# Retention followed by a SwiGLU layer on one core: the first chunk's pieces in another order, and the normalised rows written a slot ahead of their transposes

## Chip, core and metric

The kernel runs on one core of a Trainium2 chip. The metric is device time in microseconds (us) of one launch, lower is better. Engines are named as in the profile: PE (TensorE matmul), PEld (its weight load), DVE (VectorE), ACT (ScalarE), POOL (GpSimd), SP (SyncE, which here only issues transfers).

## What is computed

```python
def _attn_ref(q, k, v):                      # 4 batches, 8 heads, 768 positions, 64 wide
    for t in range(S):
        state = gamma * state + einsum('bhd,bhe->bhde', k[:, :, t], v[:, :, t])
        y[:, :, t] = scale * einsum('bhd,bhde->bhe', q[:, :, t], state)
...
x = y.transpose(0, 2, 1, 3).reshape(B * S, H * D)          # 3072 x 512
xn = x / sqrt(mean(x * x) + 1e-6) * rms_g
out = (silu(xn @ w_gate) * (xn @ w_val)) @ w_out           # 512 -> 1536 -> 512
```

All inputs and the output are float32; the kernel multiplies in bf16.

## The kernel before

The sequence is cut into 6 chunks of 128 positions. For each chunk c there are two kinds of work. The **attention pieces** run once for each of the 4 batches b:

- `cast` (line 132): q and k to bf16 (`qb`, `kb`), v times a decay (`vp`). In chunk 0 `qb` is made by ACT (line 139), in the others by POOL (line 141); `kb` and `vp` are POOL's (lines 142 and 143).
- `piece_t`: eight PE transposes into the PSUM tile `qk_ps`, one ACT copy to `qkT` (line 158).
- `piece_a`: eight matmuls into two PSUM tiles `a_ps`, two DVE multiplications by the causal mask into `am` (line 172).
- `piece_y`: the matmuls for `y_ps` and for the state's increment `kv_ps`, the DVE multiplication that gives `x` (line 199), ACT's square sum `xsq` (line 203), POOL's `ms` and `rstd` (lines 220 and 223), and the state: in chunk 0 ACT copies it to `st_f` (line 212), later DVE adds to it (line 214); POOL casts it to `st_b` (line 215).
- `piece_x`: DVE writes `xn` (line 229), PE transposes it into `xt_ps` (line 232), DVE multiplies by `g_col` into `xnT` (line 233).

The **feed-forward slots** of chunk c are 16: slots 0 to 11 are `gv(n)` (four matmuls into `g_ps`, line 264, four into `v_ps`, line 267, ACT's silu `sg`, line 269, DVE's product `hT`, line 270), slots 12 to 15 are `down(b)` (twelve matmuls into `o_ps`, line 275, ACT's copy `o_sb`, line 278, a transfer out on SP, line 279). Below, FFN(c) is this stage for chunk c, and g(n) is slot n's first matmul.

The order on every engine is the order in which the program is written: nothing is rescheduled. Chunk 0's pieces come first, in the order of a string of steps (letters C, T, A, Y, X with a batch number). Then, in each slot of FFN(c), the table `PLAN` says which pieces of chunk c+1 follow that slot's own work (`PLAN1` for chunk 1):

```python
PLAN = dict(cast=(0, 2, 4, 6), t=(1, 3, 5, 7), a=(2, 4, 6, 8), y=(3, 5, 7, 9), x=(9, 11, 13, 14))
```

Transfers in: q, k and v of one chunk and batch are three transfers of 256 KB on SP (`load`, line 64), twelve for a chunk. Chunk 0's are issued first of all; chunk 1's four groups each wait for the silu of slot 0 to 3 of FFN(0) (line 269's result, `mark`); chunk 2's follow chunk 1's on SP, and only behind them stands the first transfer out. The weights come in bf16 through POOL's queue: four pairs of 384 KB transfers for `wg_b` and `wv_b` (`load_w`, lines 122 and 123; a pair serves three slots) and three of 512 KB for `wo_b` (`load_wo`, line 127). Before, pair 0 is issued behind batch 1's cast, pair 1 behind batch 2's, pair 2 behind batch 3's, pair 3 and `wo_b` after all of chunk 0's pieces but the last `X`. Eight matmuls into a tile `hot` (line 298) stand ahead of that last `X`.

Of the kernel before, what the change touches and what calls it, by code (L numbers as in the profile page):

```python
# [17 lines left out]
def kernel(  # L18
# [11 lines left out]
    nc = tc.nc  # L30
# [3 lines left out]
    C = 128  # L34
# [3 lines left out]
    DFF = moe_w_gate.shape[1]  # L38
    KS = DM // 128
# [20 lines left out]
    def load(c, b, after=None):  # L60
        t = []
        for name, src in (("q_f", q), ("k_f", k), ("v_f", v)):
            x = loads.tile([128, H, D], F32, name=name)
            i = nc.sync.dma_start(  # L64
                out=x, in_=src[b].rearrange("h (c p) d -> c p h d", p=C)[c])
            if after is not None:
                tc.add_manual_dep(i.ins, after.ins.name, SYNC_DEP, reason="transfer order")
            t.append(x)
        raw[c, b] = t

    for b in range(B):
# [8 lines left out]
        out=causal, in_=causal, compare_op=ALU.is_ge, fill=0.0, base=0,  # L80
# [18 lines left out]
    warm = const.tile([128, 1], F32, name="warm")  # L99
    nc.scalar.activation(warm, zero, AF.Silu)  # L100
    g_col = const.tile([128, KS], F32, name="g_col")
    for s in range(KS):
        nc.scalar.dma_start(out=g_col[:, s:s + 1], in_=moe_rms_g[s * 128:(s + 1) * 128][:, None])


    st_f = [const.tile([128, NHP, D], F32, name=f"st_f{b}") for b in range(B)]
    st_b = [const.tile([128, NHP, 2 * D], BF16, name=f"st_b{b}") for b in range(B)]
# [22 lines left out]
    cur = {}  # L130
    mark = {}

    def cast(c, b):
        q_f, k_f, v_f = raw.pop((c, b))
        qb = work.tile([128, DM], BF16, name="qb")
        kb = work.tile([128, DM], BF16, name="kb")
        vp = work.tile([128, H, D], BF16, name="vp")
        if c == 0:
            nc.scalar.copy(qb, q_f.rearrange("p h d -> p (h d)"))  # L139
        else:  # L140
            nc.gpsimd.tensor_copy(qb, q_f.rearrange("p h d -> p (h d)"))
        nc.gpsimd.tensor_copy(kb, k_f.rearrange("p h d -> p (h d)"))  # L142
        nc.gpsimd.tensor_tensor(  # L143
            out=vp, in0=v_f, in1=vdec[:, c, :, None].to_broadcast([128, H, D]), op=ALU.mult)
        cur[c, b] = dict(qb=qb, kb=kb, vp=vp)
        if c == 0 and b > 0:
            load_w(b - 1)
        if 0 < c < NCH - 1:
            load(c + 1, b)

# [26 lines left out]
    def piece_y(c, b):  # L177
        d = cur[c, b]
        y_ps = aps.tile([128, H, D], F32, name="y_ps", tag="at")
        first = True  # L180
        for hp in range(NHP):
            for i in range(2):
                h = 2 * hp + i
                last = c == 0 and h == H - 1
                nc.tensor.matmul(y_ps[:, h, :], d["am"][:, i, hp, :], d["vp"][:, h, :],  # L185
                                 start=first, stop=last, skip_group_check=True)
                first = False
        if c > 0:
# [12 lines left out]
        xsq = work.tile([128, DM], F32, name="xsq")
        ssq = work.tile([128, 1], F32, name="ssq")
        nc.scalar.activation(xsq, x.rearrange("p h d -> p (h d)"), AF.Square,  # L203
                             accum_out=ssq)
        d["ssq"] = ssq
        piece_rstd(c, b)
        if c < NCH - 1:
            for i in range(2):
                r = slice(i * 64, i * 64 + 64)
                kv = kv_ps[r, :, i * 64:i * 64 + 64]  # L210
                if c == 0:
                    nc.scalar.copy(st_f[b][r], kv)
                else:
                    nc.vector.tensor_tensor(out=st_f[b][r], in0=st_f[b][r], in1=kv, op=ALU.add)
                nc.gpsimd.tensor_copy(st_b[b][r, :, i * 64:i * 64 + 64], st_f[b][r])  # L215
        d["x"] = x

    def piece_rstd(c, b):
        ms = work.tile([128, 1], F32, name="ms")
        nc.gpsimd.tensor_scalar(out=ms, in0=cur[c, b]["ssq"], scalar1=1.0 / DM, scalar2=1e-6,  # L220
                                op0=ALU.mult, op1=ALU.add)
        rstd = work.tile([128, 1], F32, name="rstd")
        nc.gpsimd.tensor_tensor(out=rstd, in0=ms, in1=mhalf, op=ALU.pow)  # L223
        cur[c, b]["rstd"] = rstd
# [114 lines left out]
```

## Time and profile before

| what | us |
|---|---|
| median of 3 runs (lowest to highest) | 295.89 (295.15 to 296.45) |
| the profiled execution, its own time | 295.43 |
| its span in the profile | 293.4 |
| PE busy | 242.3 (83%) |
| DVE busy | 135.3 (46%) |
| ACT busy | 105.6 (36%) |
| POOL busy | 96.1 (33%) |

The span is the stretch that the profile covers; the 2.0 us between it and the execution's own time lie around it. An engine's busy time is the sum of its instructions. In the timeline a line gives start, duration, engine, line of the program, operation, output from inputs, how many were merged, and in brackets the idle time before it on its engine with what ended it. "SPq" and "ACTq" lines are issues of transfers, not the transfers themselves.

### The profile page before, as it was taken

What the parts mean: (1) busy time and instruction counts of PE and PEld (TensorE: products, weight loads), DVE (VectorE), ACT (ScalarE), POOL (GpSimd) and SP (SyncE); (2) the same over time, 40 slices, a digit from 0 to 9 for tenths busy, and PEclk for the clock granted to TensorE, in tenths of its full rate; (3) what the DMA queues carried; (4) which work ended last, traced back from release to release, by engine and by line L of the source; (5) the groups of instructions that cost most, each with busy time, mean ns of one, the idle gap of its engine ahead of it and who ended that gap; (6) DMA issues with size and microseconds to landing.
All of it is one profiled execution on the core that took longest, in us unless ns stands there. A gap on an engine that the chain in (4) does not pass through costs nothing.

```text
span 293.4 us, 4497 instructions
## 1 busy us (share of the span) xinstructions
PE 242.3 (83%) x1673; PEld 123.9 (42%) x1704; DVE 135.3 (46%) x224; ACT 105.6 (36%) x199; POOL 96.1 (33%) x184
## 2 busy tenths in 40 slices
PE   0364798699939998899996899996999978999994
PEld 0243443255514544345443445443454434444441
DVE  0156433266634757326676426576324665224300
ACT  8255233243323463123642124642135432233311
POOL 6457620364270462600653400654301611000000
PEclk9999999799969999999999999999999999999999
DMA  9999699999999400028920129900120000110012
GB/s 166 208 162 122 96 175 196 231 203 216 251 198 218 74 2 0 36 91 193 221 35 1 38 107 223 209 2 0 68 78 2 0 0 2 71 71 3 0 45 98
DMA packets 84741, 30.17 MB, mean 103 GB/s; under 512 B 76016, under 2 KB 81648, under 8 KB 84720
## 3 DMA queue, kind: packets, MB, share of 16 engines
q1 hardware_dynamic: 78336, 25.17, 42.0%
q0 software_dynamic: 5808, 4.72, 10.5%
q8 instruction: 13, 0.21, 0.3%
q10 hardware_dynamic: 576, 0.00, 0.1%
q14 instruction: 8, 0.07, 0.1%
HBM read 28.31 MB, written 6.29 MB: 118 GB/s over the span
## 4 chain that ended last, share of the span: by engine, by line
PE 51%; DVE 17%; ACT 10%; DMA 8%; issue 7%; POOL 4%; SPq 2%; ACTq 0%; DVEq 0%; POOLq 0%
PE o_ps L275 19%; PE v_ps L267 11%; PE g_ps L264 11%; DVE am L172 6%; DMA k_f<-in_k_dram 5%; ACT xsq L203 4%; DVE hT L270 4%; DVE x L199 4%; ACT qkT L158 3%; ACT sg L269 3%; PE xt_ps L232 3%; DVE xn L229 2%; DMA v_f<-in_v_dram 2%; PE qk_ps L156 2%; SPq L64 2%
## 5 line engine op out<-in xcount | busy, mean ns | idle before, releaser
L270 DVE TENSOR_TENSOR hT<-sg,v_ps 128x512 bf16<-128x512 bf16 x72 | 49.5, 688 | 86.0 <-PE v_ps L267 61.5
L264 PE MATMUL g_ps<-xnT,wg_b 128*128 128x512 bf16 x272 | 73.4, 386 | 2.8 <-DVE xnT L233 1.6
L267 PE MATMUL v_ps<-xnT,wv_b 128*128 128x512 bf16 x281 | 74.9, 385 | 0.6
L269 ACT ACTIVATE sg<-g_ps 128x512 bf16<-128x512 f32 x72 | 43.0, 597 | 60.2 <-PE g_ps L264 58.2
L275 PE MATMUL o_ps<-wo_b,hT 128*128 128x512 bf16 x281 | 63.9, 379 | 0.5 <-issue 0.2
L220 POOL TENSOR_SCALAR ms<-ssq 128x1 f32<-128x1 f32 x24 | 4.8, 202 | 123.8 <-ACT xsq L203 123.8
L267 PEld LDWEIGHTS <-wv_b 128*128 128x128 bf16 x288 | 28.5, 99 | 35.1 <-issue 1.9
L275 PEld LDWEIGHTS <-hT 128*128 128x128 bf16 x288 | 27.4, 98 | 30.4
L264 PEld LDWEIGHTS <-wg_b 128*128 128x128 bf16 x288 | 26.2, 99 | 29.0 <-issue 4.0
L172 DVE TENSOR_TENSOR am<-a_ps,causal 128x512 bf16<-128x512 f32 x48 | 30.8, 683 | 16.5 <-PE a_ps L168 16.3
L278 ACT COPY o_sb<-o_ps 128x512 f32<-128x512 f32 x24 | 14.1, 586 | 62.5 <-PE o_ps L275 58.1
L233 DVE TENSOR_TENSOR xnT<-xt_ps,g_col 128x512 bf16<-128x512 bf16 x24 | 16.6, 692 | 36.3 <-PE xt_ps L232 36.3
L203 ACT ACTIVATE xsq<-x 128x512 f32<-128x512 f32 x24 | 15.1, 630 | 43.9 <-DVE x L199 43.9
L158 ACT COPY qkT<-qk_ps 128x1024 bf16<-128x1024 bf16 x24 | 24.0, 1000 | 13.5 <-PE qk_ps L156 13.5
L143 POOL TENSOR_TENSOR vp<-v_f,vdec 128x512 bf16<-128x512 f32 x24 | 25.3, 1053 | 3.5 <-DMA v_f<-in_v_dram 3.5
L232 PE MATMUL xt_ps<-ident,xn 128*128 128x128 bf16 x96 | 10.3, 235 | 17.4 <-DVE xn L229 17.4
L156 PE MATMUL qk_ps<-ident,qb 128*128 128x128 bf16 x96 | 10.2, 234 | 15.0 <-ACT qb L139 15.0
L232 PEld LDWEIGHTS <-xn 128*128 128x128 bf16 x96 | 7.1, 105 | 24.9 <-DVE xn L229 22.2
L142 POOL CAST kb<-k_f 128x512 bf16<-128x512 f32 x24 | 15.1, 627 | 6.5 <-DMA k_f<-in_k_dram 6.4
L199 DVE TENSOR_TENSOR x<-y_ps,ydec 128x512 f32<-128x512 f32 x24 | 16.5, 686 | 1.0 <-PE y_ps L185 0.7
L229 DVE TENSOR_SCALAR xn<-x,rstd 128x512 bf16<-128x512 f32 x24 | 14.6, 609 | 4.4 <-POOL rstd L223 4.4
L215 POOL CAST st_b<-st_f 64x256 bf16<-64x256 f32 x40 | 16.2, 406 | 1.2
(41 smaller groups left out, 162.1 us busy)
## 6 DMA issues: line engine op xcount, KB each, us to landing
q_f<-in_q_dram SPq DMA_DIRECT2D x24, 256.0 KB, 5.1
k_f<-in_k_dram SPq DMA_DIRECT2D x24, 256.0 KB, 5.1
v_f<-in_v_dram SPq DMA_DIRECT2D x24, 256.0 KB, 5.1
out_dram<-o_sb SPq DMA_DIRECT2D x24, 256.0 KB, 2.0
wg_b<-in_moe_w_gate_dram POOLq DMA_DIRECT2D x4, 384.0 KB, 5.5
wv_b<-in_moe_w_val_dram POOLq DMA_DIRECT2D x4, 384.0 KB, 6.5
wo_b<-in_moe_w_out_dram POOLq DMA_DIRECT2D x3, 512.0 KB, 12.0
g_col<-in_moe_rms_g_dram ACTq DMA_DIRECT2D x4, 0.5 KB, 4.0
```

The source lines that it names most:

```text
L143: nc.gpsimd.tensor_tensor(out=vp, in0=v_f, in1=vdec[:, c, :, None].to_broadcast([128, H, D]), op=ALU.mult)
L158: nc.scalar.copy(qkT, qk_ps)
L172: nc.vector.tensor_tensor(out=am[:, i], in0=a_ps[i], in1=causal[:, None, :].to_broadcast([128, NHP, 128]), op=ALU.mult)
L199: nc.vector.tensor_tensor(out=x, in0=y_ps, in1=ydec[:, c, :, None].to_broadcast([128, H, D]), op=ALU.mult)
L203: nc.scalar.activation(xsq, x.rearrange("p h d -> p (h d)"), AF.Square, accum_out=ssq)
L229: nc.vector.tensor_scalar_mul(xn, d["x"].rearrange("p h d -> p (h d)"), d["rstd"])
L232: nc.tensor.transpose(xt_ps[:, s, :], xn[:, s * 128:(s + 1) * 128], ident)
L264: nc.tensor.matmul(g_ps, wg_b[:, s, sl], xnT[:, s, :], start=s == 0, stop=s == KS - 1)
L267: nc.tensor.matmul(v_ps, wv_b[:, s, sl], xnT[:, s, :], start=s == 0, stop=s == KS - 1)
L269: mark[c, n] = nc.scalar.activation(sg, g_ps, AF.Silu)
L270: nc.vector.tensor_tensor(out=hT[:, n, :], in0=sg, in1=v_ps, op=ALU.mult)
L275: nc.tensor.matmul(o_ps, hT[:, n, b * C:(b + 1) * C], wo_b[:, n, :], start=n == 0, stop=n == NFF - 1)
```

## The change

Five edits. (1) `g_col` comes with one transfer on POOL's queue, called in the string of steps behind batch 1's cast, instead of four on ACT's. (2) In chunk 0, `qb` is cast by DVE instead of ACT, and `st_b` is copied from PSUM by ACT instead of cast from `st_f` by POOL. (3) The weights' pairs are steps of the string: pairs 0 and 1 behind batch 2's cast, pairs 2 and 3 behind batch 3's. (4) `piece_x` is split: `piece_n` writes `xn`, `piece_x` only transposes it and writes `xnT`; in chunk 0's string and in the two tables the first stands ahead of the second, in the tables by one slot (for some batches of chunk 1 in the same one), and the pieces `x` of batches 0 to 2 stand two slots earlier than before in `PLAN`. In chunk 0's string the transposes move back too: `X0` from ahead of `Y1` to behind `A2`, `X1` from ahead of `Y2` to behind `A3`, `X2` from ahead of `Y3` to behind it. (5) The matmuls into `hot` are six, not eight. In `PLAN1` batch 0's cast moves from slot 6 to slot 5.

```diff
-    for s in range(KS):
-        nc.scalar.dma_start(out=g_col[:, s:s + 1], in_=moe_rms_g[s * 128:(s + 1) * 128][:, None])
+    def load_g():
+            nc.gpsimd.dma_start(out=g_col, in_=moe_rms_g.rearrange("(s p) -> p s", p=128))
...
         if c == 0:
-            nc.scalar.copy(qb, q_f.rearrange("p h d -> p (h d)"))
+            nc.vector.tensor_copy(qb, q_f.rearrange("p h d -> p (h d)"))
...
-        if c == 0 and b > 0:
-            load_w(b - 1)
...
                 if c == 0:
+                    nc.scalar.copy(st_b[b][r, :, i * 64:i * 64 + 64], kv)
                     nc.scalar.copy(st_f[b][r], kv)
                 else:
                     nc.vector.tensor_tensor(out=st_f[b][r], in0=st_f[b][r], in1=kv, op=ALU.add)
-                nc.gpsimd.tensor_copy(st_b[b][r, :, i * 64:i * 64 + 64], st_f[b][r])
+                    nc.gpsimd.tensor_copy(st_b[b][r, :, i * 64:i * 64 + 64], st_f[b][r])
...
-    def piece_x(c, b):
-        d = cur.pop((c, b))
+    def piece_n(c, b):
+        d = cur[c, b]
         xn = work.tile([128, DM], BF16, name="xn")
         nc.vector.tensor_scalar_mul(xn, d["x"].rearrange("p h d -> p (h d)"), d["rstd"])
+        d["xn"] = xn
+    def piece_x(c, b):
+        xn = cur.pop((c, b))["xn"]
...
-    PLAN = dict(cast=(0, 2, 4, 6), t=(1, 3, 5, 7), a=(2, 4, 6, 8), y=(3, 5, 7, 9), x=(9, 11, 13, 14))
-    PLAN1 = dict(cast=(6, 7, 9, 11), t=(7, 9, 11, 13), a=(8, 10, 12, 14), y=(9, 11, 13, 15), x=(13, 14, 15, 15))
+    PLAN = dict(cast=(0, 2, 4, 6), t=(1, 3, 5, 7), a=(2, 4, 6, 8), y=(3, 5, 7, 9), n=(6, 8, 10, 13), x=(7, 9, 11, 14))
+    PLAN1 = dict(cast=(5, 7, 9, 11), t=(7, 9, 11, 13), a=(8, 10, 12, 14), y=(9, 11, 13, 15), n=(12, 14, 15, 15), x=(13, 15, 15, 15))
...
-    for step in "C0 T0 C1 A0 T1 Y0 C2 A1 T2 X0 Y1 C3 A2 T3 X1 Y2 A3 X2 Y3".split():
+    for step in ("C0 T0 C1 G0 A0 T1 Y0 C2 W0 W1 A1 T2 Y1 N0 C3 W2 W3 A2 X0 T3 Y2 N1 A3 X1 Y3 N2 X2").split():
         P[step[0]](0, int(step[1]))
-    for i in range(3, DFF // WB):
-        load_w(i)
     for i in range(3):
         load_wo(i)
     hot = fps.tile([128, GT], F32, name="hot", tag="ff")
-    for i in range(8):
+    for i in range(6):
         nc.tensor.matmul(hot, ident, st_b[0].rearrange("p a b -> p (a b)"), start=True, stop=True)
+    piece_n(0, 3)
     piece_x(0, 3)
```

The order on POOL in chunk 0, from batch 1's `vp` on. Before:

```order
L143 TENSOR_TENSOR vp<-v_f,vdec 128x512
L122 DMA wg_b<-in_moe_w_gate_dram 128x4x384
L123 DMA wv_b<-in_moe_w_val_dram 128x4x384
L220 TENSOR_SCALAR ms<-ssq 128x1
L223 TENSOR_TENSOR rstd<-ms,mhalf 128x1
L215 CAST st_b_146<-st_f_142 64x4x64 x2
L142 CAST kb<-k_f 128x512
L143 TENSOR_TENSOR vp<-v_f,vdec 128x512
L122 DMA wg_b<-in_moe_w_gate_dram 128x4x384
L123 DMA wv_b<-in_moe_w_val_dram 128x4x384
```

And with the change:

```order
L146 TENSOR_TENSOR vp<-v_f,vdec 128x512
L105 DMA g_col<-in_moe_rms_g_dram 128x4x1
L222 TENSOR_SCALAR ms<-ssq 128x1
L225 TENSOR_TENSOR rstd<-ms,mhalf 128x1
L145 CAST kb<-k_f 128x512
L146 TENSOR_TENSOR vp<-v_f,vdec 128x512
L125 DMA wg_b<-in_moe_w_gate_dram 128x4x384
L126 DMA wv_b<-in_moe_w_val_dram 128x4x384
L125 DMA wg_b<-in_moe_w_gate_dram 128x4x384
L126 DMA wv_b<-in_moe_w_val_dram 128x4x384
```

The first pair of weights has moved behind batch 2's `vp` and the second pair directly behind it; the casts of `st_b` are gone from POOL, and `g_col`'s transfer is new there. Behind these rows come batch 1's `ms` and `rstd`, batch 3's `kb` and `vp`, and pairs 2 and 3 in the same way.

The order on DVE in slots 6 to 9 of FFN(2), where chunk 3's batches 2 and 3 pass through (`am`, `x`, `st_f` are theirs, the `xn` and `xnT` those of batches 0 and 1). Before:

```order
L270 TENSOR_TENSOR hT<-sg,v_ps 128x512
L172 TENSOR_TENSOR am<-a_ps_1756,causal 128x512
L172 TENSOR_TENSOR am<-a_ps_1757,causal 128x512
L270 TENSOR_TENSOR hT<-sg,v_ps 128x512
L199 TENSOR_TENSOR x<-y_ps,ydec 128x512
L214 TENSOR_TENSOR st_f_144<-st_f_144,kv_ps 64x256 x2
L270 TENSOR_TENSOR hT<-sg,v_ps 128x512
L172 TENSOR_TENSOR am<-a_ps_1849,causal 128x512
L172 TENSOR_TENSOR am<-a_ps_1850,causal 128x512
L270 TENSOR_TENSOR hT<-sg,v_ps 128x512
L229 TENSOR_SCALAR xn<-x,rstd 128x512
L233 TENSOR_TENSOR xnT<-xt_ps,g_col 128x4x128
```

And with the change:

```order
L276 TENSOR_TENSOR hT<-sg,v_ps 128x512
L231 TENSOR_SCALAR xn<-x,rstd 128x512
L173 TENSOR_TENSOR am<-a_ps_1753,causal 128x512
L173 TENSOR_TENSOR am<-a_ps_1754,causal 128x512
L276 TENSOR_TENSOR hT<-sg,v_ps 128x512
L239 TENSOR_TENSOR xnT<-xt_ps,g_col 128x4x128
L200 TENSOR_TENSOR x<-y_ps,ydec 128x512
L216 TENSOR_TENSOR st_f_140<-st_f_140,kv_ps 64x256 x2
L276 TENSOR_TENSOR hT<-sg,v_ps 128x512
L231 TENSOR_SCALAR xn<-x,rstd 128x512
L173 TENSOR_TENSOR am<-a_ps_1854,causal 128x512
L173 TENSOR_TENSOR am<-a_ps_1855,causal 128x512
```

Batch 0's `xn` now stands ahead of batch 2's masks and its `xnT` ahead of batch 2's `x`; batch 1's `xn` and `xnT` stand in the same way in slots 8 and 9, where before they came in slot 11.

## Rows read from the trace of the kernel before

**Rows 1.** Windows: stretch, busy time of each engine, granted clock, DMA share, GB/s.
```profile
1.90:13.40 11.50, 1.22 (x12) 0.96 (x14) 0.00 (x0) 6.67 (x22) 7.19 (x15) 1.00 1.30 216
...
20.60:23.20 2.60, 1.78 (x24) 1.32 (x22) 2.08 (x4) 1.86 (x4) 1.89 (x4) 1.00 0.10 6
23.20:33.20 10.00, 5.66 (x51) 4.17 (x53) 5.57 (x9) 4.26 (x11) 6.30 (x12) 1.00 1.09 157
33.20:36.80 3.60, 2.82 (x13) 1.18 (x12) 1.29 (x2) 0.67 (x2) 3.38 (x7) 1.00 0.11 3
36.80:51.00 14.20, 13.42 (x65) 6.02 (x64) 5.50 (x8) 4.78 (x8) 2.54 (x4) 1.00 1.18 187
51.00:77.00 26.00, 22.01 (x182) 11.90 (x187) 13.12 (x23) 9.82 (x17) 12.99 (x23) 0.93 1.17 214
```

**Rows 2.** Timeline, end of FFN(0) and start of FFN(1).
```profile
76.69 2.76 PE L275 MATMUL o_ps<-wo_b,hT 128*128 128x512 bf16 x12
...
77.14 5.04 SPq L279 DMA_DIRECT2D out_dram<-o_sb  x4
...
81.23 0.59 ACT L278 COPY o_sb<-o_ps 128x512 f32<-128x512 f32 x1 [4.41 <-DMA out_dram<-o_sb]
...
85.50 0.58 PE L264 MATMUL g_ps<-xnT,wg_b 128*128 128x512 bf16 x1 [0.78 <-DVE xnT L233]
```

**Rows 3.** Waits of PE from 86 to 260 us: total, times, longest.
```profile
PE xt_ps L232 <- DVE xn L229: 11.4, 8, 2.4
```

**Rows 4.** Timeline, chunk 0: ACT and what it hands over.
```profile
8.75 1.61 ACTq L103 DMA_DIRECT2D g_col<-in_moe_rms_g_dram  x2
...
10.41 0.62 ACT L139 CAST qb<-q_f 128x512 bf16<-128x512 f32 x1 [3.41 <-DMA v_f<-in_v_dram]
...
17.30 0.74 ACT L212 COPY st_f<-kv_ps 64x256 f32<-64x256 f32 x2
...
18.29 0.93 POOL L215 CAST st_b<-st_f 64x256 bf16<-64x256 f32 x2
```

**Rows 5.** Timeline, slots 8 to 11 of FFN(2): masks, xn, transposes.
```profile
153.23 1.28 DVE L172 TENSOR_TENSOR am<-a_ps,causal 128x512 bf16<-128x512 f32 x2
...
155.09 0.48 DVE L229 TENSOR_SCALAR xn<-x,rstd 128x512 bf16<-128x512 f32 x1
155.63 0.40 PE L232 MATMUL xt_ps<-ident,xn 128*128 128x128 bf16 x4 [1.25 <-DVE xn L229]
155.86 0.40 PE L185 MATMUL y_ps<-vp,am 128*128 128x64 bf16 x8
156.06 0.69 DVE L233 TENSOR_TENSOR xnT<-xt_ps,g_col 128x512 bf16<-128x512 bf16 x1 [0.49 <-PE xt_ps L232]
```

**Rows 6.** Timeline, chunk 0: batch 3's cast on POOL, the last weights, start of FFN(0).
```profile
23.43 0.56 POOL L223 TENSOR_TENSOR rstd<-ms,mhalf 128x1 f32<-128x1 f32 x1
...
24.95 0.61 POOL L142 CAST kb<-k_f 128x512 bf16<-128x512 f32 x1
25.53 1.04 POOL L143 TENSOR_TENSOR vp<-v_f,vdec 128x512 bf16<-128x512 f32 x1
...
32.04 2.34 PE L298 MATMUL hot<-st_b,ident 128*128 128x512 bf16 x5 [0.22 <-issue]
...
34.93 0.81 POOL L122 DMA_DIRECT2D wg_b<-in_moe_w_gate_dram  x1
...
35.75 0.75 POOL L123 DMA_DIRECT2D wv_b<-in_moe_w_val_dram  x1
36.08 1.02 PE L264 MATMUL g_ps<-xnT,wg_b 128*128 128x512 bf16 x4 [0.78 <-DVE xnT L233]
```

**Rows 7.** Instructions that write xn, whole span: count, least, median, most ns.
```profile
L229 DVE TENSOR_SCALAR xn<-x,rstd x24: 477/538/1251, 18.4 to 253.8; 128x512 bf16<-128x512 f32 x24
```

**Rows 8.** Timeline, slot 11 of FFN(2): POOL's vp beside DVE's xn.
```profile
161.16 1.04 POOL L143 TENSOR_TENSOR vp<-v_f,vdec 128x512 bf16<-128x512 f32 x1
161.23 1.25 DVE L229 TENSOR_SCALAR xn<-x,rstd 128x512 bf16<-128x512 f32 x1
```

More of the change, by code (lines that the diff above doesn't have):

```diff
@@ L101 @@
     g_col = const.tile([128, KS], F32, name="g_col")
-    for s in range(KS):
-        nc.scalar.dma_start(out=g_col[:, s:s + 1], in_=moe_rms_g[s * 128:(s + 1) * 128][:, None])
+    def load_g():
+        with nc.allow_non_contiguous_dma(reason="one column per 128 entries"):
+            nc.gpsimd.dma_start(out=g_col, in_=moe_rms_g.rearrange("(s p) -> p s", p=128))
     st_f = [const.tile([128, NHP, D], F32, name=f"st_f{b}") for b in range(B)]
@@ L247, in attention @@
         plan = PLAN1 if c == 1 else PLAN
-        pieces = dict(cast=cast, t=piece_t, a=piece_a, y=piece_y, x=piece_x)
+        pieces = dict(cast=cast, t=piece_t, a=piece_a, y=piece_y, n=piece_n, x=piece_x)
         for b in range(B):
@@ L288 @@
     begin(0)
-    P = dict(C=cast, T=piece_t, A=piece_a, Y=piece_y, X=piece_x)
-    for step in "C0 T0 C1 A0 T1 Y0 C2 A1 T2 X0 Y1 C3 A2 T3 X1 Y2 A3 X2 Y3".split():
+    P = dict(C=cast, T=piece_t, A=piece_a, Y=piece_y, N=piece_n, X=piece_x, W=lambda c, i: load_w(i), G=lambda c, i: load_g())
+    for step in ("C0 T0 C1 G0 A0 T1 Y0 C2 W0 W1 A1 T2 Y1 N0 C3 W2 W3 A2 X0 T3 Y2 N1 A3 X1 Y3 N2 X2").split():
         P[step[0]](0, int(step[1]))
-    for i in range(3, DFF // WB):
-        load_w(i)
     for i in range(3):
```

## The prediction

> **What bounds the kernel now.** I read the transfers' share of each stretch first, then the waits that end last at each stage's edge, then PE's waits in the later chunks.
>
> The first 77 us are a stream of transfers. While the stream runs it moves 187 to 216 GB/s, and in two stretches it stands still: from 20.6 to 23.2 at 6 GB/s and from 33.2 to 36.8 at 3 GB/s, with a thinner stretch of 157 GB/s between them [rows 1]. That stream, not PE, sets the start of FFN(1): SP issues the first transfer out, which stands behind chunk 2's last transfer in, at 77.14; the fourth copy to `o_sb` needs that one's buffer and starts at 81.23 after 4.41 us of waiting, though PE's last `o_ps` ended at 79.45 (76.69 + 2.76); behind that copy on ACT stand the last batch's square sum and so its `rstd`, `xn`, `xnT`, and g(0) of FFN(1) at 85.50 [rows 2]. So FFN(1) moves as the stream moves, as long as PE's own path stays ahead of it.
>
> From there on PE is the bound, and its largest wait is for `xn`: 11.4 us in 8 waits, two in each of FFN(1) to FFN(4) [rows 3]. The first of each pair is about 1.25 us, which leaves 6.4 for the second ones.
>
> **The change, part by part.**
>
> *The head of ACT's queue.* ACT's first cast of `qb` starts at 10.41, just as its last two issues of `g_col` end (8.75 + 1.61 = 10.36) [rows 4]. With one transfer on POOL and the cast on DVE, chunk 0's first transposes no longer stand behind them. The four casts, 0.62 us each on ACT, cost on DVE between 0.48 (its `xn`, the same size and types) and 0.69 (its product `xnT`) [rows 5]; I take 0.5 by the nearer row. On POOL the new issue costs about what a weight's does, 0.75 to 0.81 [rows 6]. Per batch POOL loses the two casts of `st_b` (0.93), and ACT, which copied `st_f` in 0.74, copies twice as much, so +0.74 [rows 4]. All this lies in front of FFN(0) and counts only through its start.
>
> *Start of FFN(0).* Chunk 0's twelve transfers of 0.262 MB still come at 216 GB/s from 1.9 us on [rows 1]: batch 2's nine are there at about 1.9 + 10.9 = 12.8, taken as 13.9 with the time to land. Then POOL does batch 2's `vp` (1.04), pairs 0 and 1 (twice 0.81 + 0.75 = 3.1), `ms` and `rstd` (0.56 for the second, about 0.8 for both), batch 3's `kb` (0.61) and `vp` (1.04): ends at 20.5. Before, that `vp` ended at 25.53 + 1.04 = 26.57 and FFN(0) began 9.5 later, at 36.08 [rows 6]. The steps in these 9.5 are the same in kind (issue of a pair, two `rstd`, `xn`, transposes, `hot`), now with two pairs instead of one (+1.6) and two `hot` fewer (2.34 / 5 = 0.47 each, -0.9). So FFN(0) starts at 20.5 + 9.5 + 0.7 = 30.7, some 5 us earlier. This is not what I book.
>
> *The stream.* Pair 0 is now issued at about 15, while chunk 0's last transfers still run, and pair 1 follows directly: 1.57 MB (pairs of 0.786) at 187 GB/s last to 23.4. Pairs 2 and 3 are issued from 20.5, before the first two are through, and last to 32; `wo_b` is issued at 27 to 30, before that. Chunk 1's transfers wait for the silu of slot 0, at about 32.5, while `wo_b` is under way. So neither gap has a place left. At 187 GB/s the two gaps are worth 2.6 x (1 - 6/187) = 2.5 and 3.6 x (1 - 3/187) = 3.5, and the thin stretch 10.0 x (1 - 157/187) = 1.6 [rows 1]: 7.6 us. Lower bound 6.0 (the gaps alone), upper bound 9.4 (if what follows runs at 214 instead of 187 as well, 14.2 x 27/214 = 1.8 more). I take **7.6**, since 187 is the rate of the weights themselves.
>
> Does PE's path stay ahead? From FFN(0)'s start to FFN(1)'s it took 85.50 - 36.08 = 49.4, of which 81.23 - 79.45 = 1.8 was the wait for the transfer alone. From 30.7 that gives 30.7 + 47.6 = 78.3 at worst, and 77.9 is what the stream allows (85.5 - 7.6). The path also holds waits for chunk 1's transfers, which now land earlier by more than FFN(0) does, so it should come in below. The margin is thin.
>
> *Cast of chunk 1's batch 0 a slot earlier, `n` and `x` in `PLAN1`:* nothing, they end in the same wait at FFN(0)'s end; were the stream faster still, that cover would go and DVE's three transposed batches in slot 15 would come next, about 0.7 each.
>
> *`xn` ahead of its transposes, chunks 2 to 5.* The transposes find `xn` ready, and the eight waits go. But DVE now does `xn` (0.48) ahead of the masks of batch 2 and `xnT` (0.69, spaced 0.61) ahead of its `x`, then `xn` again ahead of batch 3's masks. These stand in a ring: masks, `y_ps`, `x`, square sum, the copy to `qkT` behind it on ACT, the next `a_ps`, the next masks. So batch 3's masks, which ended at 153.23 + 1.28 = 154.51, end at 154.51 + 0.5 + 0.6 + 0.5 = 156.1; `y_ps`, which waited behind the transposes until 155.86, can then start at 156.1 [rows 5]. The first wait of each pair is paid back in full, plus 0.2. The second goes, but the transposes still follow an `xn` that stands behind its slot's `hT`, some 0.2 late. So each FFN gains its second wait less 0.45: 6.4 - 4 x 0.45 = **4.6** us.
>
> The bounds: a gain of 11.4 if the work ahead of the masks costs nothing, and a loss if each of those two `xn` meets POOL's `vp`: one that did took 1.25 instead of 0.48 and ended with it [rows 8]. Twice 0.77 in four FFNs is 6.2, against 4.6 a loss of 1.6. I stay near the middle because such meetings are few: the median `xn` took 0.538 [rows 7].
>
> *The lock between DVE and POOL.* One `xn` waited until POOL's `vp` had ended [rows 8]. The new DVE casts and `xn` stand beside POOL's weight issues in chunk 0, which no row of before shows. If an issue and such a cast hold each other up by that same 0.77, a few meetings delay FFN(0) by 1 to 3 us. The Trainium skill, page "SBUF — State Buffer", section "SBUF: two separate sides", goes further and speaks against this change: a float32 copy inside SBUF on DVE locks POOL out of its port, so that a transfer issued there, about 620 ns alone, takes about 3100. By its figure, an estimate from that page, eight issues would cost 20 us more, FFN(0) would start near 51, and the kernel would take about 304. Nothing in the trace of before shows that size; the `xn` above shows only that the later one waits for the earlier.
>
> *Sum.* 295.43 - 7.6 - 4.6 = 283.2 for the profiled execution. It stood 0.46 below the median of the runs, so **283.7**.
>
> **The rivals.**
>
> - *DVE takes the second gain.* The chain in slots 6 to 9 grows by more than a microsecond in each FFN and nothing of the 4.6 is left. For it: batch 2 and 3's `am` and `x` are on the ring, and each gets DVE work put in front. Against it: 2.4 us of the longest wait lie in slot 11, behind the ring. Time 295.9 - 7.6 = 288.3.
> - *The stream's gaps close only in part.* Pairs 2 and 3 are issued behind batch 3's `vp`; if that ends later than 23.4, the stream stands again, a microsecond for each, and a late FFN(0) brings PE's path to the front in the same way. For it: the margins are 3 us and under 1. The gain then is about 4: 295.9 - 4 - 4.6 = 287.3.
> - *Slower: the port lock.* The eight issues of weights on POOL are held up by DVE's casts and `xn`, and batch 3's `kb`, `vp` and two `rstd` stand behind them. FFN(0) starts 8 d later than 30.7 if each issue grows by d. With PE's path of 49.4 - 1.8 behind it and the 4.6 still gained, the kernel is slower than before from 30.7 + 8d + 47.6 > 85.5 + 4.6, that is d over 1.5 us, an issue of 2.3 instead of 0.8 [rows 6]. At d = 2 it is 295.9 + 4.2 = 300.1. The Trainium skill's rule above is this case at d = 2.5. Against it: the 0.77 seen [rows 8] is half of what decides, and DVE has only three casts and two `xn` among the issues.
> - *The change does nothing:* only if gaps and waits come back elsewhere in full; I see no place.
>
> **How the numbers follow.** The forecast has 0.66 (within 279 to 286), DVE's chain 0.15, the partial stream 0.13, the lock 0.04, nothing 0.02. The range reaches down to 279.0, where the stream gives 9.4 and the second part 7.5 of its 11.4, and up to 289.5, past both milder rivals with 1 us of their own bounds. Beyond lie the lock and the tails of the others, under 2 in 10. About 0.5% (1.5 us) is what a measurement of this kernel can tell from no change: faster 0.94, same 0.02, slower 0.04.
>
> **What would show it.** Right: no stretch under 100 GB/s between 3 and 65 us; FFN(0) near 31; the first transfer out issued near 69.5; FFN(1) near 78; one short wait for `xn` in each later FFN, with `y_ps` of batch 3 as late against g(9) as before. Wrong: weight issues on POOL over 1.5 us (the lock); a standing stream around 24 (late pairs); PE waits for `am` of over half a microsecond in slots 7 and 9 (DVE's chain); FFN(1) not earlier than 82.

## The result and the profile after

| | before | changed |
|---|---|---|
| median of 4 runs, us | 296.07 (295.15 to 296.45) | **280.31** (279.49 to 280.64) |
| profiled execution, its span | 295.43, 293.4 | 279.49, 277.8 |
| FFN(0) to FFN(5) start at | 36.08, 85.50, 129.99, 173.57, 216.15, 258.39 | 29.43, 76.31, 119.38, 160.35, 201.32, 242.94 |

The ratio is 0.947, with a 95% interval of 0.944 to 0.950: faster by 15.8 us, 3.4 us below the forecast and inside its range. Of the kernels run later, one execution of `e2_old_weight_steps` (286.60) fell into a slower state and is left out of its time. The starts (g(0) of each stage, from the timeline) split it: FFN(1) begins 9.19 us earlier, where the stream term had 7.6. The stages FFN(1) to FFN(4) are shorter by 1.42, 2.61, 1.61 and 0.62, together 6.26, where the `xn` term had 4.6.

The windows of the changed kernel, in the stretches of [rows 1] as far as its stream goes (columns as there):

```profile
1.90:13.40 11.50, 4.97 (x48) 3.26 (x48) 4.46 (x8) 8.60 (x27) 7.46 (x17) 1.00 1.27 219
20.60:23.20 2.60, 1.81 (x17) 0.95 (x15) 2.32 (x5) 2.50 (x7) 2.60 (x4) 1.00 1.33 208
23.20:33.20 10.00, 8.35 (x35) 3.84 (x36) 3.71 (x8) 2.65 (x8) 4.18 (x8) 1.00 1.31 202
33.20:36.80 3.60, 3.60 (x18) 1.65 (x17) 1.52 (x3) 1.19 (x2) 0.00 (x0) 1.00 1.23 202
36.80:51.00 14.20, 13.90 (x96) 6.98 (x94) 6.78 (x11) 5.09 (x8) 4.54 (x6) 1.00 1.15 213
51.00:67.00 16.00, 15.56 (x132) 8.09 (x130) 9.57 (x19) 7.72 (x14) 9.32 (x18) 1.00 1.07 213
```

The last column is the reading: no stretch stands still. 6, 157 and 3 GB/s have become 208, 202 and 202, and 187 has become 213. The table leaves out 13.4 to 20.6 us; the thinnest two microseconds in it, 16 to 18, have 145 GB/s.

The timeline of the changed kernel where FFN(0) ends, against [rows 2]:

```profile
66.54 2.76 PE L281 MATMUL o_ps<-wo_b,hT 128*128 128x512 bf16 x12
...
67.93 5.04 SPq L285 DMA_DIRECT2D out_dram<-o_sb  x4
...
71.75 0.68 DVE L200 TENSOR_TENSOR x<-y_ps,ydec 128x512 f32<-128x512 f32 x1
72.02 0.59 ACT L284 COPY o_sb<-o_ps 128x512 f32<-128x512 f32 x1 [5.12 <-DMA out_dram<-o_sb]
...
76.31 1.87 PE L270 MATMUL g_ps<-xnT,wg_b 128*128 128x512 bf16 x4 [0.78 <-DVE xnT L239]
```

The first transfer out is issued 9.21 us earlier (77.14 to 67.93), and FFN(1) follows by the same amount. PE's last `o_ps` ends at 69.30, but the fourth copy still waits for a buffer until 72.02. (The 5.12 in its bracket is all the time that ACT stood idle before it.)

Its timeline in chunk 0, against [rows 4, 6]:

```profile
4.13 0.43 DVE L142 CAST qb<-q_f 128x512 bf16<-128x512 f32 x1 [4.13 <-DMA q_f<-in_q_dram]
...
6.91 0.99 ACT L159 COPY qkT<-qk_ps 128x1024 bf16<-128x1024 bf16 x1
...
14.76 0.82 POOL L125 DMA_DIRECT2D wg_b<-in_moe_w_gate_dram  x1
...
15.43 0.48 DVE L231 TENSOR_SCALAR xn<-x,rstd 128x512 bf16<-128x512 f32 x1
15.59 0.96 POOL L126 DMA_DIRECT2D wv_b<-in_moe_w_val_dram  x1
15.83 0.42 DVE L142 CAST qb<-q_f 128x512 bf16<-128x512 f32 x1
...
19.48 1.03 POOL L146 TENSOR_TENSOR vp<-v_f,vdec 128x512 bf16<-128x512 f32 x1
...
29.43 1.86 PE L270 MATMUL g_ps<-xnT,wg_b 128*128 128x512 bf16 x4 [0.78 <-DVE xnT L239]
```

Two things: the first weights are issued at 14.76, and an issue beside DVE's `xn` and cast takes 0.96, not several microseconds.

PE's waits from 86 to 260 us in the kernel before, beside those of [rows 3], then from 76 to 244 us in the changed kernel, and all its `xn`, against [rows 7]:

```profile
PE a_ps L168 <- ACT qkT L158: 2.0, 6, 0.5
PE y_ps L185 <- DVE am L172: 1.3, 8, 0.2
```

```profile
PE a_ps L169 <- ACT qkT L159: 3.9, 9, 0.7
PE y_ps L186 <- DVE am L173: 3.8, 13, 0.4
...
PE xt_ps L238 <- DVE xn L231: 0.3, 2, 0.2
```

```profile
L231 DVE TENSOR_SCALAR xn<-x,rstd x24: 475/486/1362, 15.4 to 233.3; 128x512 bf16<-128x512 f32 x24
```

The 11.4 us of waits for `xn` are down to 0.3. The waits for `qkT` and for the masks, 2.0 and 1.3 before, are 3.9 and 3.8: part of the gain was paid back there.

### The profile page after: what moved, and what is told of

The parts are those of the page before. It is cut to its first block, busy times and chain, and to the rows that moved or that the text cites. A ratio compares the mean times of both kernels' runs of the same rounds, so it can differ in the third digit from the quotient of the medians.

```text
span 277.8 us, 4510 instructions
## 1 busy us (share of the span) xinstructions
PE 246.2 (89%) x1702; PEld 124.4 (45%) x1702; DVE 135.7 (49%) x228; ACT 105.3 (38%) x203; POOL 94.5 (34%) x177
## 4 chain that ended last, share of the span: by engine, by line
PE 51%; DVE 15%; ACT 9%; DMA 8%; POOL 6%; issue 6%; SPq 3%; ACTq 0%; POOLq 0%; DVEq 0%
PE o_ps L281 21%; PE g_ps L270 13%; PE v_ps L273 12%; DVE am L173 5%; DMA k_f<-in_k_dram 4%; DVE hT L276 3%; SPq L64 3%; ACT xsq L204 3%; DVE x L200 3%; ACT qkT L159 3%; ACT sg L275 3%; DVE xn L231 2%; DMA v_f<-in_v_dram 2%; DVE xnT L239 2%; PE xt_ps L238 2%
## 5 line engine op out<-in xcount | busy, mean ns | idle before, releaser
L270 PE MATMUL g_ps<-xnT,wg_b 128*128 128x512 bf16 x288 | 76.3, 388 | 1.6 <-DVE xnT L239 1.6
L273 PE MATMUL v_ps<-xnT,wv_b 128*128 128x512 bf16 x288 | 75.7, 386 | 0.0
L144 POOL CAST qb<-q_f 128x512 bf16<-128x512 f32 x20 | 12.8, 640 | 15.0 <-DMA q_f<-in_q_dram 14.1
L186 PE MATMUL y_ps<-vp,am 128*128 128x64 bf16 x192 | 13.1, 202 | 4.5 <-DVE am L173 4.5
L169 PE MATMUL a_ps<-qkT 64*128 64x128 bf16 x192 | 10.4, 233 | 6.7 <-ACT qkT L159 6.1
L231 DVE TENSOR_SCALAR xn<-x,rstd 128x512 bf16<-128x512 f32 x24 | 15.6, 649 | 1.1 <-POOL rstd L225 1.1
```

The costliest lines, as they stand in the source:

```text
L270: nc.tensor.matmul(g_ps, wg_b[:, s, sl], xnT[:, s, :], start=s == 0, stop=s == KS - 1)
L273: nc.tensor.matmul(v_ps, wv_b[:, s, sl], xnT[:, s, :], start=s == 0, stop=s == KS - 1)
```

## The experiments

Twelve kernels ran, each beside the kernel before on the same chip. All but one start from the changed kernel; times are medians, to be set against 280.31. The kernel before took 295.04 to 296.07 in the four groups of runs, so a difference of 1 us between times of different groups is not told apart; the ratio is to the kernel before of the same group.

**The old slots for `xn`** (`e1_old_plan`): everything but the split in `PLAN` and the two slots that `x` moved with it.

```diff
-    PLAN = dict(..., n=(6, 8, 10, 13), x=(7, 9, 11, 14))
+    PLAN = dict(..., n=(9, 11, 13, 14), x=(9, 11, 13, 14))
```

> The changed kernel, but in chunks 2 to 5 xn is written in the same slot as its transposes, in the slots of before (9, 11, 13, 14). If the split of xn is worth what FFN(1) to FFN(4) lost in length between the two traces (44.5 to 43.1, 43.6 to 41.0, 42.6 to 41.0, 42.2 to 41.6, together 6.3 us), this takes 280.3 + 6.3 = 286.6 and the two waits for xn stand in each of these stages again. If those stages became shorter for another reason (transfers out of the way, POOL's queue shorter), it takes under 283.

285.38 (284.60 to 286.24), ratio 0.964 [0.961, 0.968]. FFN(1) starts at 76.81, nearly as in the changed kernel; the four stages after it are 4.63 us longer (0.81, 1.60, 1.60, 0.62), which is the forecast's 4.6. Its waits of PE from 76 to 244 us:

```profile
PE xt_ps L238 <- DVE xn L231: 10.3, 8, 1.4
PE a_ps L169 <- ACT qkT L159: 2.0, 6, 0.5
PE y_ps L186 <- DVE am L173: 1.3, 8, 0.2
```

The eight waits are back, the other two as before. But the longest is 1.4, not 2.4: the `xn` that stood behind POOL's `vp` in FFN(2) of before [rows 8] does so no longer, and that stage alone is 1.01 shorter than before. So this microsecond of the 6.26 came with the other edits, not with the split; how, the runs do not show. FFN(1) is another 0.61 shorter than before. Its clock differs as well, as the windows of the first 10 us from g(0) show, first the changed kernel, then this one, then the kernel before:

```profile
76.30:86.30 10.00, 9.99 (x51) 4.26 (x51) 3.26 (x5) 3.30 (x5) 3.18 (x5) 0.78 1.19 216
```

```profile
76.80:86.80 10.00, 9.99 (x68) 4.89 (x68) 3.88 (x7) 3.30 (x5) 3.38 (x5) 0.86 1.31 220
```

```profile
85.50:95.50 10.00, 9.78 (x56) 4.43 (x57) 3.30 (x6) 3.30 (x5) 3.16 (x5) 0.81 1.35 220
```

A granted clock of 0.78 instead of 0.86 over 10 us is 0.8 us of work at the full rate. With that taken out, the split is worth about 1.6 in each of FFN(1) to FFN(3). In the same way 0.86 against 0.81 is 0.5 of the 0.61.

**The weights' steps.** First the old places of the weights in the changed kernel (`e2_old_weight_steps`), then the new places alone, put into the kernel before (`e3_new_weight_steps_alone`).

```diff
-    for step in ("C0 T0 C1 G0 A0 T1 Y0 C2 W0 W1 A1 T2 Y1 N0 C3 W2 W3 A2 X0 T3 Y2 N1 A3 X1 Y3 N2 X2").split():
+    for step in ("C0 T0 C1 W0 G0 A0 T1 Y0 C2 W1 A1 T2 Y1 N0 C3 W2 A2 X0 T3 Y2 N1 A3 X1 Y3 N2 X2 W3").split():
```

> The changed kernel, with the weights' pairs at their steps of before (pair 0 behind batch 1's cast, 1 behind batch 2's, 2 behind batch 3's, 3 at the end of chunk 0's steps). Theory one, the order of the issues closed the gaps: the stream stands again once or twice, FFN(1) starts 3 to 7 us later, 283 to 287. Theory two, chunk 0's faster pieces closed them: POOL reaches the later pairs while the earlier ones still run, no stretch falls under 100 GB/s, and the time is within 1 us of 280.3.

282.06 (281.60 to 284.78), ratio 0.958 [0.951, 0.964]: slower by 1.8 by the medians and 3.2 by the ratios, with FFN(1) at 78.76, 2.45 later. In its windows the stream thins:

```profile
24.00:28.00 4.00, 2.88 (x22) 1.68 (x20) 3.25 (x7) 2.40 (x8) 2.49 (x7) 1.00 1.06 127
28.00:32.00 4.00, 3.22 (x12) 1.32 (x10) 1.04 (x2) 0.23 (x1) 3.65 (x5) 1.00 1.01 150
```

From 24 to 26 us alone it has 65 GB/s: thinner than theory two allowed, but no standstill as in theory one. Pair 0 is issued at 11.24, 3.5 us *earlier* than in the changed kernel, and runs beside chunk 0's last loads. Pair 2 stands on POOL behind batch 3's `vp`, which now waits for its `v_f` and starts 2.76 later than in the changed kernel (19.48):

```profile
22.24 1.04 POOL L146 TENSOR_TENSOR vp<-v_f,vdec 128x512 bf16<-128x512 f32 x1 [2.97 <-DMA v_f<-in_v_dram]
```

That the early weights delayed these loads fits, but was not tried apart.

Then the edit for the new places alone:

```diff
-        if c == 0 and b > 0:
-            load_w(b - 1)
+        if c == 0 and b > 1:
+            load_w(2 * b - 4)
+            load_w(2 * b - 3)
...
-    for i in range(3, DFF // WB):
-        load_w(i)
```

> The kernel before, with only the weights' issues moved: pairs 0 and 1 behind batch 2's cast, 2 and 3 behind batch 3's. If the stream of transfers alone sets the start of FFN(1), it starts 7 to 9 us earlier and the kernel takes 287 to 289. If PE's path through chunk 0 and FFN(0) is as near as the forecast had it (FFN(0) no earlier than 36, and 47.6 us less the wait for chunk 1's first transfers from there to FFN(1)), FFN(1) starts 2 to 5 us earlier and the kernel takes 291 to 294.

293.44 (293.12 to 293.93) against 295.75 of the kernel before beside it, ratio 0.992 [0.989, 0.995]. The order of the weights alone is worth 2.3 us, less than either theory had, and not 7.6. The timeline has POOL's first weight issue, and the windows what stands until then:

```profile
21.06 0.97 POOL L122 DMA_DIRECT2D wg_b<-in_moe_w_gate_dram  x1
```

```profile
16.00:20.00 4.00, 1.65 (x18) 0.92 (x15) 2.58 (x4) 2.03 (x6) 2.08 (x5) 1.00 0.18 29
20.00:23.00 3.00, 2.43 (x28) 1.97 (x28) 1.66 (x3) 1.45 (x2) 3.00 (x5) 1.00 0.13 4
23.00:40.00 17.00, 9.88 (x70) 5.84 (x71) 7.31 (x13) 5.93 (x15) 12.90 (x23) 1.00 1.27 190
```

Both old gaps are closed, and a new one has opened ahead of the first weights, which now stand behind batch 2's casts, and these behind batch 0's `ms`, for which POOL stands idle 6.36 us until ACT's square sum. FFN(0) starts at 37.96, 1.88 *later* than before, and FFN(1) at 83.75, 1.75 *earlier*.

**The edits of chunk 0, each undone alone:** the casts of `qb` on ACT again (`e7_qb_on_act`), the casts of `st_b` on POOL (`e8_stb_on_pool`), the four transfers of `g_col` on ACT (`e9_gcol_on_act`).

```diff
-            nc.vector.tensor_copy(qb, q_f.rearrange("p h d -> p (h d)"))
+            nc.scalar.copy(qb, q_f.rearrange("p h d -> p (h d)"))
```

> The changed kernel with chunk 0's qb cast on ACT as before. ACT gets 4 x 0.62 us and cannot cast batch 0 before its table loads end at 7.0 instead of 4.1. If FFN(0)'s start decides little and POOL's chain with batch 3 sets it, FFN(0) is later by under 0.7 and the time by under 0.7: 280.3 to 281. If the cast on DVE was what brought FFN(0) forward, it is 2 us or more.

```diff
-                    nc.scalar.copy(st_b[b][r, :, i * 64:i * 64 + 64], kv)
+                    nc.gpsimd.tensor_copy(st_b[b][r, :, i * 64:i * 64 + 64], st_f[b][r])
```

> The changed kernel with chunk 0's st_b cast on POOL from st_f as before (0.93 us for each batch). POOL's chain rstd, kb, vp, issues gets two such casts ahead of batch 3's kb, and one more ahead of the last rstd. If that chain sets FFN(0), it starts 1.9 to 2.8 us later and, PE's path being as late as the stream, the time is 1 to 2.8 up: 281.3 to 283. If the stream hides it, it is 280.3.

```diff
+    for s in range(KS):
+        nc.scalar.dma_start(out=g_col[:, s:s + 1], in_=moe_rms_g[s * 128:(s + 1) * 128][:, None])
...
-            nc.gpsimd.dma_start(out=g_col, in_=moe_rms_g.rearrange("(s p) -> p s", p=128))
+            pass
```

> The changed kernel with g_col's four transfers back on ACT's queue, at the head of its program, and none on POOL. Their issues kept ACT until 10.4 in the kernel before, so its first copy to qkT should start there instead of at 6.9, and with it batch 0's masks and rstd, which POOL meets ahead of batch 2's kb and vp and so ahead of the weights' first issue. In the runs so far FFN(1) starts 33.3 us (32.8 to 34.0) after the weights' last packet. If that is the rule, the first issue moves by 1.5 to 3 us, FFN(1) with it, and the time is 281.8 to 283.3. If the head of ACT's queue is absorbed before batch 2 arrives, it is 280.3 within 0.7.

| | time, us | ratio to before | first weight issue | FFN(0) | FFN(1) | FFN(1) less first issue |
|---|---|---|---|---|---|---|
| changed kernel | 280.31 | 0.947 [0.944, 0.950] | 14.76 | 29.43 | 76.31 | 61.6 |
| `st_b` on POOL | 281.07 | 0.951 [0.948, 0.955] | 15.85 | 31.31 | 77.59 | 61.7 |
| `qb` on ACT | 282.19 | 0.957 [0.951, 0.962] | 16.33 | 30.86 | 78.76 | 62.4 |
| `g_col` on ACT | 285.09 | 0.964 [0.960, 0.967] | 18.17 | 32.95 | 81.72 | 63.6 |
| weights' places alone | 293.44 | 0.992 [0.989, 0.995] | 21.06 | 37.96 | 83.75 | 62.7 |

The `g_col` edit is the largest of the edits in chunk 0, 4.8 us. The 0.8 of `st_b` lies within the intervals, though FFN(1) is 1.28 later there. Of the three, only `g_col` cost clearly more than was expected (1.5 to 3 us). The timeline of the kernel without the `g_col` edit, and then the same `ms` of batch 0 in the changed kernel:

```profile
8.83 1.63 ACTq L104 DMA_DIRECT2D g_col<-in_moe_rms_g_dram  x2
...
10.50 1.01 ACT L162 COPY qkT<-qk_ps 128x1024 bf16<-128x1024 bf16 x1 [3.50 <-DMA v_f<-in_v_dram]
...
15.83 0.19 POOL L225 TENSOR_SCALAR ms<-ssq 128x1 f32<-128x1 f32 x1 [4.62 <-ACT xsq L207]
...
18.17 0.97 POOL L128 DMA_DIRECT2D wg_b<-in_moe_w_gate_dram  x1
```

```profile
12.30 0.18 POOL L222 TENSOR_SCALAR ms<-ssq 128x1 f32<-128x1 f32 x1 [0.18 <-ACT xsq L204]
```

ACT's first `qkT` starts where its last issue ends, 3.6 us later than in the changed kernel (6.91), and POOL's first weights come 3.4 later. Between the two lies POOL's wait for batch 0's square sum: 0.18 us in the changed kernel, 0.19 with `st_b` on POOL (there the casts themselves delay it), 1.84 with `qb` on ACT, 4.62 here. In all five kernels of the table the weights are issued behind batch 2's casts. The first transfer out follows the first issue by 53.2 to 54.3 us, and FFN(1) by 61.6 to 63.6 us. Of the 63.6, 1.2 is another path: there the fourth copy ends at 76.76, but ACT then stands idle 1.18 us for the last batch's `x`. FFN(0) does not order them so: with `qb` on ACT it starts 0.45 us earlier than with `st_b` on POOL, but the first issue is 0.48 later there, and FFN(1) 1.17 later.

**What holds FFN(1) now.** A fourth `o_sb` buffer (`e4_four_out_buffers`) takes away the wait at 72.02.

```diff
-            o_sb = ffw.tile([128, DM], F32, name="o_sb")
+            o_sb = ffw.tile([128, DM], F32, name="o_sb", bufs=4)
```

> The changed kernel with four buffers instead of three for the output rows, so that the fourth copy of a stage no longer waits for the first transfer out. If that wait alone sets FFN(1)'s start, the copy moves from 72.0 to 69.3 and the kernel gains 2.7: 277.6. If the last batch's x, which is ready at 72.4 behind two batches of transposes in slot 15, is as late as the transfer, nothing more than 0.3 is gained: 280.0 to 280.3.

281.16 (280.55 to 282.58), ratio 0.951 [0.947, 0.954]: no gain. The timeline says why:

```profile
69.36 0.58 ACT L284 COPY o_sb<-o_ps 128x512 f32<-128x512 f32 x1 [2.44 <-PE o_ps L281]
...
71.76 0.68 DVE L200 TENSOR_TENSOR x<-y_ps,ydec 128x512 f32<-128x512 f32 x1
72.54 0.63 ACT L204 ACTIVATE xsq<-x 128x512 f32<-128x512 f32 x1 [2.60 <-DVE x L200]
```

The copy comes 2.66 us earlier, but the last batch's square sum starts when it did: its `x` stands on DVE behind the two `xnT` and the `xn` of slot 15. Two paths end together there.

Next, each slot's attention pieces emitted with all casts, transposes, masks and `y` first and all `xn` and transposes of `xn` last: alone (`e5_masks_first`), and with the fourth buffer (`e6_masks_first_four_out_buffers`).

```diff
-        for b in range(B):
-            for n, f in pieces.items():
-                s[plan[n][b]].append(lambda f=f, b=b: f(c, b))
+        for group in (("cast", "t", "a", "y"), ("n", "x")):
+            for b in range(B):
+                for n in group:
+                    s[plan[n][b]].append(lambda f=pieces[n], b=b: f(c, b))
```

> The changed kernel, but within each slot the pieces cast, t, a and y of all batches stand ahead of n and x, so that DVE does the masks and x of batches 2 and 3 before the xn and xnT of batches 0 and 1. If the xn ahead of the masks still costs about 1 us in each of FFN(1) to FFN(4) (the waits for masks and for qkT of 1.7 to 2.7 us per stage), these stages shorten by 0.7 to 1.2 each, and FFN(4) by more, since its first xn met POOL's vp: 276 to 277.5. If that work was hidden, nothing changes: within 0.5 of 280.3.

> Both of the last two edits: masks first, and four output buffers. With masks first the last batch's y of chunk 1 stands ahead of the transposes in slot 15, so if x and the transfer out were equally late in the changed kernel, both are removed only here: FFN(1) starts 1.5 to 2 us earlier than with masks first alone. If the transfer is not what holds that start, it is equal to masks first alone within 0.5.

276.30 (275.96 to 277.94) and 276.78 (275.45 to 277.24), ratios 0.936 both: faster than the changed kernel by 3.5 to 4 by the medians and 3.1 by the ratios, and the fourth buffer again adds nothing. PE's waits of the first from 76 to 244 us:

```profile
PE a_ps L169 <- ACT qkT L159: 3.8, 9, 0.6
PE y_ps L186 <- DVE am L173: 1.9, 12, 0.2
```

Half of the waits for masks are gone (3.8 to 1.9); FFN(1) to FFN(4) are shorter than in the changed kernel by 1.3, 0.5, 0.5 and 1.9, the middle two by less than the 0.7 forecast, and FFN(1) starts 0.7 *later* (77.05, and 77.35 with the fourth buffer). Of the 1.3, some 0.8 is clock: the granted clock over the first 10 us of FFN(1) is 0.86 there, against 0.78. In the second kernel PE waits once within FFN(0) for a cast of chunk 1, as it does in the first for 2.0 us (waits from 29 to 78 us):

```profile
PE qk_ps L157 <- POOL kb L145: 2.1, 1, 2.1
```

Then `wo_b` out of the way of chunk 1's loads (`e10_wo_after_first_loads`).

```diff
+        tc.add_manual_dep(d.ins, after.ins.name, SYNC_DEP, reason="transfer order")
...
-    for i in range(3):
-        load_wo(i)
...
+            if c == 0 and i == 4:
+                for j in range(3):
+                    load_wo(j, mark[0, i])
```

> The changed kernel, but the three transfers of w_out are issued after the silu of slot 4 of FFN(0), so that chunk 1's first two batches come ahead of them. The bytes of the whole stream are the same. Theory one, the end of the whole stream (chunk 2's last transfer, behind it the first transfer out) holds FFN(1): it stays at 76.3 and the time at 280.3 within 0.7. Theory two, chunk 1's first transfers hold it: kb's wait in slot 7 goes and FFN(1) is earlier by up to 1 us, no more, since that wait was only 0.3.

280.97 (280.75 to 281.41), ratio 0.950 [0.948, 0.953]: no gain. The wait for `kb` is gone, as theory two had it, but FFN(1) starts at 78.11, 1.80 later, which neither theory had. The same bytes pass ahead of the first transfer out, it is issued 1.60 later (67.93), and the fourth copy starts 1.83 later (72.02):

```profile
69.53 5.25 SPq L286 DMA_DIRECT2D out_dram<-o_sb  x4
...
73.85 0.58 ACT L285 COPY o_sb<-o_ps 128x512 f32<-128x512 f32 x1 [9.11 <-DMA out_dram<-o_sb]
```

Last, the three edits together (`e11_wo_late_masks_first_four_buffers`), and the same with eight `hot` (`e12_same_with_eight_hot`).

```diff
-    for i in range(6):
+    for i in range(8):
         nc.tensor.matmul(hot, ident, st_b[0].rearrange("p a b -> p (a b)"), start=True, stop=True)
```

> Masks first, four output buffers, and w_out after slot 4's silu. With the wait for the transfer out gone by the buffers and the 2.1 us wait for chunk 1's first kb gone by the order, PE's path is what is left before FFN(1): it starts 1.5 to 2.5 us earlier than with the first two alone (77.35 there), 274 to 275. If the stream still holds it through chunk 1's last transfers, it stays at 276 to 277.

> The same with eight matmuls into hot instead of six. In the changed kernel the first slot of FFN(0) ran at the lower of the two clocks (four matmuls in 1.86 us instead of 1.03) and FFN(0)'s last transposes waited behind hot. Two more take 0.9 and may bring the clock up before the first slot, which is worth up to 1.7: between 0.8 faster and 0.9 slower than with six, if PE's path sets FFN(1); no change if the stream does.

275.14 (272.94 to 275.99), ratio 0.929 [0.925, 0.934], and **274.21** (273.86 to 274.64), ratio 0.928 [0.925, 0.931]: equal within their intervals, and the fastest of all. FFN(1) starts at 73.33 and 73.97, with six `hot` 4.0 earlier than with the first two edits, where 1.5 to 2.5 was expected. A fourth buffer alone gained nothing, since the last batch's `x` ended as late, and a late `wo_b` alone nothing, since the fourth copy still waited for the transfer out; all three edits take 3.0 us off FFN(1)'s start. The late `wo_b` and the fourth buffer without the masks first were not tried.

## Why the prediction was right

The mechanisms were the forecast's: the gaps in the stream closed, PE's path kept ahead of it, and the waits for `xn` went at a price on DVE. Both terms came out larger than booked, and one step of the working was wrong.

- **The step that failed** is the one on ACT's head: "All this lies in front of FFN(0) and counts only through its start", with "This is not what I book" behind it. The whole 7.6 was then put down to where the weights are issued. The runs show otherwise. Undone alone, the edits on `g_col`, `qb` and `st_b` cost 4.8, 1.9 and 0.8 us, the weights' places 1.8 and the split 5.1: together 14.4 by the medians and 17.6 by the ratios, for 15.8 gained, so they do not add up exactly. The weights' places alone, without the others, gave 2.3. What the edits on `g_col`, `qb` and `st_b` move is batch 2's turn on POOL, in the first two through the wait for batch 0's square sum, and with it the *first weight issue*; where the first issue came at 21.06, the stream all but stood from 16 us on (29 and 4 GB/s), with chunk 0's own transfers through. The forecast had the first issue at about 15 and it came at 14.76; what it left out is which edits put it there. FFN(0)'s start is not the link: with the weights' places alone it came later while FFN(1) came earlier.
- **The stream term's size.** The bounds were 6.0 to 9.4 and it measured 9.2. The step mis-sized is "187 is the rate of the weights themselves": that stretch of before begins while the stream is still starting again (82 GB/s to 38.0, 196 from there on) and mixes weights with chunk 1's loads. The weights ran at 202 to 208 GB/s and the stretch from 36.8 on at 213. With 202 the two gaps and the thin stretch give 2.52 + 3.55 + 2.23 = 8.3, and the last stretch up to 14.2 x 26/213 = 1.7 more.
- **FFN(0)'s start** was forecast at 30.7 and is 29.43; batch 3's `vp` ends at 20.51 (19.48 + 1.03), forecast 20.5.
- **PE's path.** "The margin is thin" held in another place than meant: `o_ps` ends 2.7 us ahead of the copy, but the last batch's `x` on DVE ends with it, as the fourth buffer shows. That is what the forecast named as next, "DVE's three transposed batches in slot 15".
- **The `xn` term** of 4.6 is what undoing the split alone gives back, 4.63. The other 1.6 of the 6.26 is not of the split: 1.0 is the meeting of `xn` and `vp` in slot 11 of FFN(2) [rows 8], which the old slots in the changed kernel no longer have, 0.6 is in FFN(1), where the granted clock differs from kernel to kernel. That 4.6 and 4.63 agree is luck: the 4.6 counts that 1.0 as a gain of the split, and takes off 0.45 in each stage, of which FFN(2) shows less (below). The price was named rightly in kind. The timeline of FFN(2) in the changed kernel, against [rows 5]:

```profile
143.58 0.48 DVE L231 TENSOR_SCALAR xn<-x,rstd 128x512 bf16<-128x512 f32 x1
...
143.98 1.28 DVE L173 TENSOR_TENSOR am<-a_ps,causal 128x512 bf16<-128x512 f32 x2
...
144.57 0.39 PE L238 MATMUL xt_ps<-ident,xn 128*128 128x128 bf16 x4
...
145.32 0.38 PE L186 MATMUL y_ps<-vp,am 128*128 128x64 bf16 x7 [0.34 <-DVE am L173]
```

Batch 3's masks end 25.88 us after g(0) (145.26 less 119.38), 24.52 before: 1.36 later, where the working had 1.6. The transposes wait for nothing, and `y_ps` waits 0.34. Its matmuls behind that wait start 25.94 us after g(0), 25.87 before: 0.07 is paid, where the working had 0.2.

- **FFN(4) gained only 0.62.** There the first `xn`, the one ahead of batch 2's masks, meets a `vp`, as the forecast's lower bound had it for every stage; in FFN(1) to FFN(3) a meeting comes only at the last `xn`, with no masks behind it:

```profile
219.00 1.04 POOL L146 TENSOR_TENSOR vp<-v_f,vdec 128x512 bf16<-128x512 f32 x1
219.04 1.28 DVE L231 TENSOR_SCALAR xn<-x,rstd 128x512 bf16<-128x512 f32 x1
```

With the masks first no `xn` after 190.39 us takes over 0.48, and that stage is 1.9 shorter. That fits, but the masks' own gain is in the 1.9 too, and the two were not taken apart.

- **The rivals.** DVE's chain: PE does wait for masks 13 times, but never over 0.4 us, and 4.6 is left. The partial stream: the old places of the weights show it, at 2.45 us for FFN(1). The port lock: no issue of POOL among DVE's casts took over 0.97, and one took 0.97 in the kernel before too, at 11.06 us. The 1.5 us more that would have decided are nowhere. The Trainium skill's 3100 ns (page "SBUF — State Buffer", section "SBUF: two separate sides") do not appear; `wv_b` at 15.59, with `xn` and a float32 cast beside it (0.48 and 0.42 us long), took 0.96. A meeting of two computing instructions, `vp` and `xn`, does cost what [rows 8] showed, 1.28 instead of 0.48.

That the time lies inside the range is in part luck: 1.6 us that no step of the working had lowered it further, and the range, 4.7 us wide below the forecast, took up the 3.4.

Not tried alone: six against eight `hot` in the changed kernel, chunk 1's earlier cast, and the later transposes in chunk 0.

## What to carry to other kernels

Where a stream of transfers sets the time, ask of every edit ahead of it what it does to the *first* issue that must follow: a few tiny transfers at the head of one engine's queue cost 4.8 us here, handed on from ACT by PE and DVE to POOL, at the far end of the stream. Take the stream's full rate from a stretch that is full and unmixed, not from the average of the one next to the gap. Two paths that end together hide each other: a fourth buffer gained nothing alone, nor did a later `wo_b`, and the two took 3 us off FFN(1)'s start together with a third edit.

## What the runs showed of the hardware that was not expected

**Matmuls at half rate under a full granted clock.** In the changed kernel the first four and the next four matmuls of FFN(0) take 1.86 and 1.89 us, then 1.04 from 32.79 on, and the window over them grants the full clock (1.00, the level of 2.4 GHz):

```profile
29.40:33.00 3.60, 3.57 (x9) 1.25 (x9) 0.00 (x0) 0.60 (x1) 0.00 (x0) 1.00 1.31 203
```

At the start of FFN(1), where the granted clock is 0.50 from 76.3 to 78.0 (the level of 1.2 GHz), the same four take 1.87. Before those of FFN(0) PE ran six `hot`, 2.77 us for the six and so at half rate too, and four transposes, and stood idle from 28.64 to 29.43. The kernel of the three edits does the same with six `hot`, and its first four take 1.02:

```profile
29.20 1.02 PE L272 MATMUL g_ps<-xnT,wg_b 128*128 128x512 bf16 x4 [0.78 <-DVE xnT L240]
```

So the number of `hot` alone does not decide it, and what does stays open: four of the eleven kernels with six `hot` start so, none of the three with eight. It costs about 1.6 us of FFN(0) (the third group of four starts 3.36 us after the first, not 1.72). The stream hides that here: with the old slots for `xn`, the same FFN(0) starts at 29.45 at the full rate, PE then waits 2.4 us instead of 0.3 for chunk 1's first `kb`, and FFN(1) starts no earlier (76.81).

**The meeting of `xn` and `vp` costs `xn`, whichever of the two began first.** At 219.04 `xn` began 0.04 us after `vp` and took 1.28; at 109.93 it began 0.04 us *before* `vp` (109.97, 1.04) and took 1.36, and so again at 150.91. The changed kernel has one such meeting in each of FFN(1) to FFN(4). In each, `xn` ends 0.28 or 0.29 us after `vp`, and so it did in [rows 8] (162.48 against 162.20), where the forecast read that it "ended with it" and that the later one waits.
